# A gated linear recurrence feeding a two-layer perceptron: the first 512 steps as two units of 256

## The chip, the cores and the metric

The kernel runs on one core of one Trainium2 chip. The metric is the device time of one execution in microseconds (us). The engines are named as the profile names them: PE is TensorE (PEld its weight loads), DVE is VectorE, ACT is ScalarE, POOL is GpSimd, SP is SyncE; SP, ACT and POOL also issue DMAs. Each engine runs its own instructions strictly in order.

## The reference

For each of 4 sequences and 8 heads, a state of 48 x 48 complex numbers decays by a complex gate of at most 0.999 in magnitude and takes up k v^T; q reads the real part. The result, as 3072 rows of 384, goes through a perceptron with squared ReLU.

```python
mag = np.sqrt(a_re * a_re + a_im * a_im)
scale = np.minimum(mag, 0.999) / (mag + 1e-06)
a_re_n, a_im_n = (a_re * scale, a_im * scale)
for t in range(S):                      # S = 768
    new_re = ar * S_re - ai * S_im
    new_im = ar * S_im + ai * S_re
    S_re, S_im = (new_re + k v^T, new_im)
    y[t] = q[t] @ S_re
h = x @ w_in                            # x: (3072, 384), w_in: (384, 2048)
r = np.maximum(h, 0.0)
out = (r * r) @ w_out                   # w_out: (2048, 384)
```

The two weight matrices arrive as 64-bit floats and are converted on the chip.

## The kernel before

**Blocks.** The 3072 steps are six blocks of 512 (`L`). A block's gates a, and its q and k, lie in `aq[z]`, z being the half of the heads, with four consecutive steps in each of the 128 partitions. For each block the same stages follow.

1. *Chain* (`chain`). `roots` and `normalise` scale the gates (ACT: square, logarithm, exponential; DVE: the rest). `inner` multiplies up the gates of a partition's four steps, three rounds of products per half (L1006, L1014); the last product is `xn`. `totals` turns `xn` so that the partitions lie along the free dimension (PE, L1040), `scan` forms the running products over the 128 partitions (DVE, many small instructions, L1065 to L1175), and `back` turns the result back. `rest`/`apply` multiplies it into each step, takes the inverse by logarithm and exponential, and writes the scaled q and k (L1241 to L1306). In block 0 some sums of `apply` are made by PE in PSUM (`both`, table `HOMES`).
2. *Pairs* (`pairs`). For each of four pairs of heads: q and k are turned (PE transposes and ACT evictions in block 0 and for three pairs of block 1, otherwise DVE and DMA), `score` makes masked products of chunks of 128 steps (PE, DVE mask at L1443), `keep` carries the states (L1468, L1482), `mix` sums the output (L1499, L1503), which ACT and DMAs put into `xT`. `gather` brings the scaled k into chunk order by DMA (L1342).
3. *Dense* (`dense`), for two groups of 256 steps. First layer L1550 with `w1`, ReLU and square on ACT, second layer L1598 with `w2`; `(0,0)`, `(0,1)` and `(1,0)` in this plain form, later groups with seven products in place of eight (`seven`, L1660), and block 5 with a similar scheme in the first layer (`eleven`).

**Weights.** `piece`, `fetch` and `convert` bring eight raw pieces of w1 and eight of w2 (768 KB each) into whatever memory is still free (`raw1`, `raw2`), and ACT (L839, L844) and DVE (L846 to L853) convert them to 32 bits.

**Order of the work.** Every operation is a step with an engine, a duration that the program assumes, keys that it reads and writes, and a rank. `Plan` places the steps by a list schedule over all engines and emits each engine's instructions in that order; at run time each engine keeps its order and waits on semaphores. Ranks say who goes first among what is ready: chain of block n `(CHAIN, n)` = (2, n), its pairs (1, n), conversions (2, 0.3) and (2, 0.6), dense (3, n). From block 1 on the chain's and pairs' steps off DVE come ahead of everything.

The numbers that set up block 0 and the conversions:

```python
FINE = [(0, 0), (0, 1), (1, 0), (1, 1)]
BY_PE = [(0, i) for i in range(NP)] + [(1, i) for i in range(3)]
rank = (W2, 0.6) if i >= NPIECE else (W1, 0.3)
```

Of the kernel before, what the change touches and what calls it, by code (L numbers as in the profile page):

```python
# [603 lines left out]
def fast_path(ctx, tc, q, k, v, a_re, a_im, moe_w_in, moe_w_out, out, flag):  # L604
# [6 lines left out]
    C = 128  # L611
    W = 4
    L = W * C
    NU = B * S // L
# [16 lines left out]
    FINE = [(0, 0), (0, 1), (1, 0), (1, 1)]  # L631
# [6 lines left out]
    BY_PE = [(0, i) for i in range(NP)] + [(1, i) for i in range(3)]  # L638
# [55 lines left out]
    ok = sb("ok", NU * 4).rearrange("p (n j) -> p n j", n=NU)  # L694
# [37 lines left out]

    def vs(n):
        return n % 2 if n < ROOM else 0

# [29 lines left out]
    def fk(z, *qs, ps=(0, 1)):  # L765
        return [("f", z, q_, p) for q_ in qs for p in ps]
# [4 lines left out]

    CHAIN, PAIR, DENSE, CONV, LATE = 2, 1, 3, 3, 5
    W1, W2 = 2, 2

# [14 lines left out]
    def two(t):  # L789
# [9 lines left out]
    tkeys = [[("QT", 2, 0), ("QT", 2, 1)], [("QT", 2, 0), ("QT", 2, 1), ("A", 2)], [("v", 1)]]  # L799
# [3 lines left out]
    raw2 = [w2slot(3), q2, v1,  # L803
            (QT[0].bitcast(U32)[:, 0:2 * PW], [("QT", 0, 0), ("QT", 0, 1)]),
            (QT[1].bitcast(U32)[:, 0:2 * PW], [("QT", 1, 0), ("QT", 1, 1)]),
            w2slot(3), q2, v1]
# [20 lines left out]
    def convert(i):  # L827
        held = tuple(plan.wrote[("a", 1)][1]) if SOON <= i < NPIECE else ()
# [4 lines left out]
        rank = (W2, 0.6) if i >= NPIECE else (W1, 0.3)  # L833
# [22 lines left out]
    def inspect(i):  # L856
# [6 lines left out]
        if i == 0:  # L863
            step("POOL", 0.2, xk(NU - 1, range(NM)), [("gate", 1)],
                 lambda: pool.tensor_copy(out=gate[:, 0:NM],
                                          in_=xT[:, (NU - 1) % 2, :, L - 1]), rank)
# [13 lines left out]
    def parts(n):  # L880

        t, got = n * L, []
        while t < (n + 1) * L:
            b, s = divmod(t, S)
            m = min(S - s, (n + 1) * L - t)
            got.append(((t - n * L) // W, m // W, b, s))
            t += m
        return got

    def places(i):  # L890
        return [(CH, 0, CH), (0, CH, CH)] if i % 2 else [(0, 0, C)]

    def load(n):
        rank = (CHAIN, n)
        for half, name, pair in ((0, "a", (a_re, a_im)), (1, "qk", (q, k))):
            for z in range(2):
                t = aq[z][:, half * Z:(half + 1) * Z].rearrange(
                    "p (r h x) -> p r h x", r=2, h=HH)
                late = []
                if half and (n == 1 or n > 2):  # L900
                    late = xk(n - 1, [NM - 1])
                split = n == z == half == 0
                for x, j, ap in [(x, j, ap) for x in range(1 + split) for j, ap in enumerate(pair)]:
                    hs = slice(x * HH // 2, (x + 1) * HH // 2) if split else slice(0, HH)
                    for p0, m, b, s in parts(n):
                        src = ap[b, z * HH + hs.start:z * HH + hs.stop, s:s + m * W, :].rearrange(
                            "h (p c) d -> p h (c d)", c=W)
                        queue = sp if n else pool if half else (sp, act)[j]
                        dma(queue, late if n or not half else [("gate",)],
                            [(name, z)] + [(name, z, "r", j, y) for y in ([x] if split else [0, 1])  # L910
                                           if n == 0],
                            lambda t=t, p0=p0, m=m, j=j, src=src, queue=queue, hs=hs:
                            queue.dma_start(out=t[p0:p0 + m, j, hs], in_=src),
                            rank, *((m * 3072, 4.0) if n else (m * 2765 // (1 + split), 2.25)),
                            group=n)
            if n == 0 and half == 0:
                for z in range(2):
                    step("POOL", 0.2, [("a", z)], [("gate",)],
                         lambda z=z: pool.tensor_copy(out=gate[:, z:z + 1],
                                                      in_=aq[z][:, Z - 1:Z]), rank)  # L920
        t = vv[vs(n)].rearrange("p (i h d) -> p i h d", i=W, h=H)
        for i in range(W):
            b, s = divmod(n * L + i * C, S)
            src = v[b, :, s:s + C, :].rearrange("h t d -> t h d")
            vrank = (CHAIN, 1) if n == 1 else (DENSE, 20 + n if n else 6)
            for p0, t0, m in places(i):
                dma(pool, [("gate", 2)] if n == 2 else xk(n - (vs(n) == vs(n - 1)), [NM - 1])
                    if n else [("gate",)],
                    [("v", vs(n))], lambda i=i, p0=p0, t0=t0, m=m, src=src: pool.dma_start(
                        out=t[p0:p0 + m, i], in_=src[t0:t0 + m]), vrank,  # L930
                    m * 1536 * (1 if n else 1.9), 4.0 if n else 2.9, group=n)

    def chain(n):
# [89 lines left out]
        if n == 0:  # L1023
            fill(FILLS[0], ("a", 1))
# [934 lines left out]
```

## Time and profile before

| | |
|---|---|
| runs of the kernel | 668.84 and 669.37 us, median 669.11 |
| the profiled execution | 669.86 us; span 668.1 us from first to last instruction |
| granted TensorE clock, mean | 0.975 |
| busy: PE, DVE, ACT, POOL | 630.8, 574.1, 347.3, 116.8 us |
| PE waits in the first 44 us | 16.8, 9.1 and 2.8 us, each for DVE's `xn` |
| first dense matmuls of block 0, steady from | 84.7 us |
| first dense matmuls of block 1 | 192.1 us |
| DMA | 80.35 MB, 120 GB/s on average |

Busy times of engines overlap; an engine that is not the bottleneck may idle at no cost. PE's busy time includes short gaps between matmuls, since matmul ends are modelled, and each 32-bit matmul stands as two records (a transpose as one). In a row of the timeline stand the start, the busy time of the group, the engine, the line and operation, out<-in, the shapes and the count; in brackets the idle time ahead of it and what ended it.

### The profile page before, as it was taken

The page shows a single profiled execution, that of the slowest core. Times are in us where ns is not written, and L with a number is a line of the kernel's source. Part 1 is how long each engine was busy: PE and PEld are TensorE (multiplying, and loading weights), DVE is VectorE, ACT ScalarE, POOL GpSimd, SP SyncE. Part 2 cuts the span into 40 slices and gives each one's busy share as a digit, 9 for nine tenths or more (in the row PEclk, how much of TensorE's full clock was granted, in tenths as well). Part 3 has the DMA queues.
Part 4 walks back from the last instruction along what each step waited for, and adds up shares of the span by engine and source line. Part 5 has one row for each costly group of instructions (what it writes and reads, how often), then busy time and mean ns, then how long its engine had stood idle before and what let it go on. Part 6 is the DMA issues. An engine that isn't in the chain of part 4 may idle for free.

```text
span 668.1 us, 11941 instructions
## 1 busy us (share of the span) xinstructions
PE 630.8 (94%) x4414; PEld 551.9 (83%) x4414; DVE 574.1 (86%) x1147; ACT 347.3 (52%) x600; POOL 116.8 (17%) x192
## 2 busy tenths in 40 slices
PE   3259999999999999999999999999999999999996
PEld 3237886787778689999988999988999989988996
DVE  7999997898798898798989898989879989659971
ACT  7948979775656262448353358263367352045400
POOL 7401040402000021040021040111040111032200
PEclk8569999999999999999999999999999999999999
DMA  6963686305530037560057580056470053377720
GB/s 194 322 239 69 147 248 154 71 1 156 135 90 1 12 87 186 131 174 6 7 129 174 132 179 0 14 118 164 122 178 1 25 123 95 81 228 239 255 95 29
DMA packets 54340, 80.35 MB, mean 120 GB/s; under 512 B 11200, under 2 KB 36896, under 8 KB 54272
## 3 DMA queue, kind: packets, MB, share of 16 engines
q0 software_dynamic: 15360, 42.51, 22.7%
q1 hardware_dynamic: 34448, 31.64, 18.5%
q10 hardware_dynamic: 4464, 5.35, 3.2%
q8 instruction: 37, 0.61, 0.4%
q14 instruction: 31, 0.25, 0.1%
HBM read 48.76 MB, written 4.72 MB: 80 GB/s over the span
## 4 chain that ended last, share of the span: by engine, by line
PE 91%; DVE 5%; ACT 1%; DMA 1%; issue 0%; SPq 0%; DVEq 0%
PE d L1550 29%; PE d L1660 25%; PE d L1598 9%; PE sc L1440 5%; PE tr L1468 4%; PE yp L1499 4%; PE yp L1503 3%; PE d L1795 2%; PE tr L1795 2%; PE sc L1550 2%; PE sc L1795 1%; PE tr L1040 1%; DMA aq<-in_a_re_dram 1%; PE d L1419 1%; PE tr L1419 1%; PE yp L1795 1%
## 5 line engine op out<-in xcount | busy, mean ns | idle before, releaser
L1550 PE MATMUL d<-xT,w 128*128 128x256 f32 x888 | 198.7, 381 | 0.0
L1550 PEld LDWEIGHTS d<-xT,w 128*128 128x128 f32 x888 | 166.7, 190 | 23.3 <-issue 0.7
L1583 ACT ACTIVATE g<-d 128x512 f32<-128x512 f32 x74 | 44.2, 598 | 90.8 <-PE d L1550 84.8
L1660 PE MATMUL d<-T,g 128*128 128x192 f32 x512 | 88.7, 328 | 0.0
L1660 PEld LDWEIGHTS d<-T,g 128*128 128x128 f32 x512 | 83.2, 190 | 1.1 <-issue 0.7
L1615 POOL DMA_DIRECT2D out_dram<-ot x40 | 25.6, 643 | 259.5 <-DVE ot L1685 162.3
L1660 PE MATMUL d<-w,g 128*128 128x192 f32 x384 | 68.1, 329 | 0.0
L1598 PE MATMUL d<-w,g 128*128 128x384 f32 x192 | 64.9, 489 | 0.0
L1660 PEld LDWEIGHTS d<-w,g 128*128 128x128 f32 x384 | 62.3, 190 | 1.5 <-issue 0.9
L1342 POOL DMA_DIRECT2D KC<-f x52 | 28.1, 557 | 151.8 <-DVE f L1306 124.8
L1598 PEld LDWEIGHTS d<-w,g 128*128 128x128 f32 x192 | 35.6, 190 | 22.1 <-issue 0.2
L1584 ACT ACTIVATE g<-g 128x512 f32<-128x512 f32 x80 | 50.6, 633 | 2.6
L1676 DVE TENSOR_TENSOR g<-g 128x512 f32<-128x512 f32 x64 | 43.2, 685 | 7.0 <-PE d L1660 6.3
L1241 DVE TENSOR_TENSOR f<-aq,xn 128x384 f32<-128x384 f32 (+1 forms) x64 | 46.0, 752 | 1.8 <-ACT xn L1186 1.8
L1393 DVE STREAM_TRANSPOSE aq<-f 128x384 f32<-128x384 f32 (+1 forms) x51 | 42.7, 914 | 0.3
L1440 PEld LDWEIGHTS sc<-QT 96*64 96x64 f32 x736 | 33.3, 137 | 5.1 <-issue 3.2
L1006 DVE TENSOR_TENSOR f<-aq 128x384 f32<-128x384 f32 x72 | 37.0, 554 | 0.6
L1440 PE MATMUL sc<-QT 96*64 96x128 f32 (+1 forms) x736 | 36.7, 250 | 0.2 <-ACT QT L1423 0.2
L1443 DVE TENSOR_TENSOR A<-sc,mask 128x512 f32<-128x512 f32 x45 | 29.7, 683 | 7.4 <-PE sc L1440 7.2
L1685 DVE TENSOR_TENSOR ot<-ot,d 128x192 f32<-128x192 f32 x63 | 21.3, 350 | 14.5 <-PE d L1660 14.0
L1272 ACT ACTIVATE f<-aq 128x1536 f32<-128x1536 f32 (+1 forms) x14 | 16.9, 1208 | 24.5 <-DVE aq L1258 24.4
L1499 PE MATMUL yp<-A,v 128*48 128x128 f32 x312 | 29.6, 277 | 0.0
(274 smaller groups left out, 1107.9 us busy)
## 6 DMA issues: line engine op xcount, KB each, us to landing
QT<-aq SPq DMA_DIRECT2D x136, 64.0 KB, 2.0
f<-in_moe_w_in_dram POOLq DMA_DIRECT2D x8, 768.0 KB, 6.3
f<-in_moe_w_out_dram POOLq DMA_DIRECT2D x8, 768.0 KB, 6.7
QT<-aq ACTq DMA_DIRECT2D x68, 64.0 KB, 2.1
out_dram<-ot POOLq DMA_DIRECT2D x40, 96.0 KB, 3.6
KC<-f POOLq DMA_DIRECT2D x36, 96.0 KB, 3.5
xT<-yt SPq DMA_DIRECT2D x34, 96.0 KB, 2.8
T<-in_moe_w_out_dram POOLq DMA_DIRECT2D x4, 768.0 KB, 11.2
```

The lines of the kernel that those rows point to most:

```text
L1006: lambda c=c, j=j: dve.tensor_tensor(out=f[:, j], in0=a[:, :, :, c - 1], in1=a[:, j, :, c].unsqueeze(1).to_broadcast([C, 2, HH, D]), op=AL ...
L1241: lambda j=j, r=r: dve.tensor_tensor(out=f4[:, j, r], in0=a[:, r], in1=over(j), op=ALU.mult), rk)
L1393: lambda src=src, dst=dst: dve.transpose(out=dst, in_=src), rank)
L1440: pe.matmul(sa[p0:p0 + CH, j, t0:], lhsT=T[:, j, 1, h, t0:t0 + CH], rhs=T[:, j, 0, h, t0:], start=True, stop=True)
L1499: pe.matmul(ps[64 * h:64 * h + D, j - js[0]], lhsT=v5[:, j, 2 * i + h], rhs=aa[h][:, j], start=True, stop=at[j] is None)
L1550: pe.matmul(ps, lhsT=w1[:, f // FP, m, ts(f % FP, C)], rhs=xT[:, n % 2, m, ts(grp, G)], start=(m == 0), stop=(m == NM - 1))
L1583: act.activation(out=o, in_=ps, func=AF.Relu)
L1584: act.activation(out=o, in_=o, func=AF.Square)
L1598: pe.matmul(ps, lhsT=gt[:, f % 2, ts(i, C)], rhs=w2[:, f], start=(f == 0), stop=(f == NF - 1))
L1660: pe.matmul(bank[b][:, 0:DH], lhsT=gsets[x][h][:, j - HW * h, r], rhs=w(j), start=first and j == 0, stop=last and j == NT - 1)
L1676: lambda: dve.tensor_tensor(out=g[:, :, o], in0=g[:, :, x0], in1=g[:, :, x1], op=op),
L1795: pe.matmul(ps[:, jj], lhsT=u[:, ts(jj, C)], rhs=v_, start=i == 0, stop=i == len(terms) - 1)
```

## The change

Block 0 becomes two *units*, 0 and 1, of 256 steps; blocks 1 to 5 are units 2 to 6. `UNITS` holds each unit's first step and its steps per partition, 2 for the first two units and 4 for the others. Unit 0 and unit 1 each have their own loads, roots, products in the lanes (one round in place of three), totals, scan, turning back, apply, turns, scores and states, all of half width but for the totals, the scan and the turning back, whose tiles do not depend on the unit's length. Only unit 0 has PSUM homes. Loads of a, q and k read runs of two steps (384 bytes) in place of four (768). Dense group (0,0) follows unit 0's pairs, group (0,1) those of unit 1; the groups keep their 256 steps. Block 1's roots keep two of their columns in `TT`, so that they needn't wait for `ff`.

The raw w2 pieces 3 and 4 go to the second half of `xT` and the second third of `TT` in place of `QT[0]` and `QT[1]`, and w2's conversions get the rank (2, 0.12), that is ahead of unit 1's chain.

```diff
+    R1, R2 = 0.3, 0.12
+    UNITS = [(0, 2), (L // 2, 2)] + [(L * i, W) for i in range(1, NB)]
+    NU = len(UNITS)
+    FIRST_ = 2
-    FINE = [(0, 0), (0, 1), (1, 0), (1, 1)]
+    FINE = [(0, 0), (0, 1), (1, 0), (1, 1), (2, 0), (2, 1)]
-    BY_PE = [(0, i) for i in range(NP)] + [(1, i) for i in range(3)]
+    BY_PE = [(n, i) for n in range(FIRST_) for i in range(NP)] + [(2, i) for i in range(3)]
...
     raw2 = [w2slot(3), q2, v1,
-            (QT[0].bitcast(U32)[:, 0:2 * PW], [("QT", 0, 0), ("QT", 0, 1)]),
-            (QT[1].bitcast(U32)[:, 0:2 * PW], [("QT", 1, 0), ("QT", 1, 1)]),
-            w2slot(3), q2, v1]
+            (xT[:, 1].rearrange("p m t -> p (m t)").bitcast(U32), xk(1, range(NM))),
+            q3, w2slot(3), q2, v1]
...
-        rank = (W2, 0.6) if i >= NPIECE else (W1, 0.3)
+        rank = (W2, R2) if i >= NPIECE else (W1, R1)
...
+    def home_of(n):
+        w = UNITS[n][1]
+        z = 2 * HH * w * D
+        return w, z, z // 2, 2 * z * n if n < FIRST_ else 0
...
     def chain(n):
-        rank = (CHAIN, n)
-        A = [aq[z][:, 0:Z] for z in range(2)]
+        u = blk(n)
+        W, Z, Y, off = home_of(n)
+        rk0 = (0, 0.15)[n] if n < FIRST_ else u
+        rank = (CHAIN, rk0)
+        A = [aq[z][:, off:off + Z] for z in range(2)]
...
+        away = n == FIRST_
+        if away:
+            for z in range(2):
+                col[z][2:] = [TT[:, (2 * z + x) * Y:(2 * z + x + 1) * Y] for x in range(2)]
...
-        spare = ["sc0", "sc1", "tr0", "tr1"][:4 - 2 * n] if n < EARLY and grp == 0 else []
+        spare = ["sc0", "sc1"] if n < EARLY and grp == 0 else []
...
-        for grp in range(2):
-            (seven if n == NU - 1 else dense)(n, grp)
+        for grp in [n] if n < FIRST_ else range(2):
+            (seven if u == NB - 1 else dense)(u, grp)
```

How it moves instructions is shown at two places. The first is PE around the totals of block 1, the transposes of `xn` by `perm` (L1040 before, L1098 now; L1598 and L1684 are the second layer, L1550 and L1636 the first, L1588 and L1592 `mix`). Before:

```order
L1598 MATMUL d_113<-w_67,g 128x384 x2
L1598 MATMUL d_111<-w_67,g 128x384 x2
L1040 MATMUL tr_116<-perm,xn 128x16x8 x3
L1040 MATMUL tr_117<-perm,xn 128x16x8 x3
L1598 MATMUL d_111<-w_67,g 128x384 x2
L1550 MATMUL d_112<-xT,w_66 128x256 x3
```

Now:

```order
L1684 MATMUL d_112<-w_67,g 128x384 x2
L1588 MATMUL yp<-A_87,v_78 48x128
L1588 MATMUL yp<-A_88,v_78 48x128
L1592 MATMUL yp<-QT_75,S_86 48x128 x2
L1588 MATMUL yp<-A_87,v_78 48x128
L1588 MATMUL yp<-A_88,v_78 48x128
L1592 MATMUL yp<-QT_75,St_90 48x128 x2
L1636 MATMUL d_110<-xT,w_66 128x256 x6
L1636 MATMUL d_111<-xT,w_66 128x256 x3
L1098 MATMUL tr_115<-perm,xn 128x16x8 x3
L1098 MATMUL tr_116<-perm,xn 128x16x8 x3
```

Before, the totals stand inside the second layer of group (0,0), of which two matmuls are left. Now that layer stands between unit 1's pairs and is used up, then come unit 1's last `mix`, nine matmuls of group (0,1), and the totals.

The second place is DVE at the end of unit 1's scan (L1221, L1226), which didn't exist before (L866, L870 and L873 convert a raw piece, out<-raw; L1301 is the first row of unit 1's apply):

```order
L866 TENSOR_SCALAR w_66<-xT 128x768
L873 ISA w_66<-xT,w_66 128x1536
```

and ten rows on:

```order
L873 ISA w_66<-T,w_66 128x1536
L866 TENSOR_SCALAR w_67<-xT 128x768
L873 ISA w_67<-w_67 128x1536
L866 TENSOR_SCALAR w_67<-T 128x768
L870 SCALAR_TENSOR_TENSOR w_67<-T,w_67 128x768
L873 ISA w_67<-T,w_67 128x1536
L1301 TENSOR_TENSOR f_70<-aq_68,xn 128x192 x5
```

`w_66` is w1 and `w_67` w2. The raw piece of w1 in `xT` is converted inside the scan, and twelve rows later a raw piece of w2 is read from the same place; conversions of w2, which stood between block 1's roots before, stand ahead of unit 1's apply.

More of the change, by code (lines that the diff above doesn't have):

```diff
@@ L942, in chain @@
-        ahead = (CHAIN, n - 0.01)
-        late = [rank, (CHAIN, n + 0.1) if n == 0 else rank]
+        u = blk(n)
+        W, Z, Y, off = home_of(n)
+        rk0 = (0, 0.15)[n] if n < FIRST_ else u
+        early = n < FIRST_
+        rank = (CHAIN, rk0)
+        A = [aq[z][:, off:off + Z] for z in range(2)]
+        QK = [aq[z][:, off + Z:off + 2 * Z] for z in range(2)]
+        fu = [f[:, off:off + 2 * Z] for f in ff]
+        col = [[fu[z][:, s * Y:(s + 1) * Y] for s in range(4)] for z in range(2)]
@@ new lines, in chain @@
+        key = partial(fk, n=n)
+        away = n == FIRST_
+        if away:
+            for z in range(2):
+                col[z][2:] = [TT[:, (2 * z + x) * Y:(2 * z + x + 1) * Y] for x in range(2)]
+        room = [("QT", 2, h, x) for h in range(2) for x in range(2)] + [("A", 2, x) for x in range(2)]
+        room = room * away
+        first = (CHAIN, 0.25) if u == 1 else (CHAIN, rk0 - 0.02) if early else rank
+        ahead = (CHAIN, rk0 - 0.01)
+        late = [rank, (CHAIN, rk0 + 0.1) if early else rank]
@@ L1120, in side @@
         def side(n_, src, reads, dst, writes, after=()):
-            if n:
+            if not early:
                 step("DVE", tt(n_), reads, writes, lambda: dve.tensor_copy(out=dst, in_=src), ahead,
```

326 lines of the change are left out of this document (189 added, 137 removed).

## The prediction

> **What bounds the kernel now.** First the page: its second line of busy times and the slices, to see which engine is full and where it is not.
>
> ```profile
> PE 630.8 (94%) x4414; PEld 551.9 (83%) x4414; DVE 574.1 (86%) x1147; ACT 347.3 (52%) x600; POOL 116.8 (17%) x192
> PE   3259999999999999999999999999999999999996
> DVE  7999997898798898798989898989879989659971
> ```
>
> TensorE (PE) is full from the fourth slice on (16.7 us each), VectorE (DVE) from the first. So the span is a start in which DVE works and PE mostly waits, then about 600 us of PE. Next the waits of PE in the whole run, which say what the start consists of:
>
> ```profile
> PE tr L1040 <- DVE xn L1014: 19.6, 2, 16.8
> PE tr L1040 <- DVE xn L1168: 9.3, 2, 9.1
> ```
>
> Both are waits for DVE's first chain: roots and products of block 0 (L1014), then its scan (L1168). After them PE waits for nothing longer than 0.7 us before the kernel's last 30 us. Third, the busy times by stretches (PE, PEld, DVE, ACT, POOL; the second figure of each "busy (x)" is a count):
>
> ```profile
> 30.70:43.00 12.30, 3.23 (x21) 2.80 (x19) 11.32 (x42) 8.32 (x15) 2.93 (x4) 0.78 1.03 313
> 43.00:77.10 34.10, 32.89 (x320) 26.20 (x321) 33.47 (x78) 26.51 (x48) 4.35 (x8) 0.93 0.36 90
> 77.10:103.40 26.30, 26.30 (x191) 22.94 (x188) 25.82 (x43) 21.57 (x33) 9.22 (x12) 1.00 0.85 221
> 103.40:125.60 22.20, 22.20 (x76) 13.78 (x75) 17.93 (x27) 19.26 (x29) 2.99 (x4) 1.00 0.39 103
> 125.60:160.00 34.40, 34.40 (x176) 27.30 (x175) 32.19 (x94) 22.85 (x46) 6.31 (x11) 1.00 0.21 46
> ```
>
> DVE is full up to 103 us and nearly so to 160, while PE is full too from 43 on. The two meet at four places, read in the timeline:
>
> ```profile
> 84.71 1.99 PE L1550 MATMUL d<-xT,w 128*128 128x256 f32 x8
> 125.01 0.63 DVE L1014 TENSOR_TENSOR xn<-f 128x192 f32<-128x192 f32 x2
> 125.31 0.88 PE L1040 MATMUL tr<-perm,xn 128*128 128x128 f32 x6
> 192.13 2.86 PE L1550 MATMUL d<-xT,w 128*128 128x256 f32 x12
> ```
>
> Dense work runs steadily from 84.71. DVE ends block 1's products xn at 125.6, and PE turns them at 125.31, half of them before the other half is written: DVE arrives just in time. From there PE is busy without a gap to 192.13, where block 1's own dense layer begins. So up to 125.3 the start has two bounds of the same height, and DVE has this slack in it:
>
> ```profile
> 106.99 0.96 DVE L973 SCALAR_TENSOR_TENSOR f<-f 128x768 f32<-128x768 f32 x1 [3.56 <-ACT f L968]
> ```
>
> **The change, part by part.** It halves the latency to the first dense matmul and adds DVE work ahead of block 1's xn. Both are worked out.
>
> *What comes earlier.* Block 0's xn needs, with half the steps, the same instructions at half the width. One of 384 elements starts 0.47 us after the last, one of 192 0.27 us (the fence below); the first chain ends at 28.1 now. By the new order the DVE rows to unit 0's xn sum to 12.6 us against 23.2 at the same place now, that is 17.5 us with the same 4.9 us of landings and waits around them. Its scan then ends at about 36 instead of 42.98 (unit 1's roots stand between its rows), and its apply, at half width, at about 57 instead of 77.1. First dense matmuls come near 60, steady ones near 64: 20 us earlier than 84.7.
>
> *What is added on DVE.* The rows that carry it:
>
> ```profile
> 27.53 0.63 DVE L1014 TENSOR_TENSOR xn<-f 128x192 f32<-128x192 f32 x2
> 76.62 0.55 DVE L1306 TENSOR_TENSOR f<-aq 128x384 f32<-128x384 f32 x1
> 20.32 1.96 DVE L1006 TENSOR_TENSOR f<-aq 128x384 f32<-128x384 f32 x4
> 22.20 0.90 DVE L1014 TENSOR_TENSOR aq<-f 128x192 f32<-128x192 f32 x3
> 30.68 0.13 DVE L1065 MEMSET e<- 128x3 f32 x2
> 38.83 0.55 DVE L846 TENSOR_SCALAR w<-g 128x768 uint32<-128x768 uint32 x1
> 42.98 0.54 DVE L1241 TENSOR_TENSOR f<-aq,xn 128x384 f32<-128x384 f32 x1
> 45.94 1.49 DVE L1241 TENSOR_TENSOR f<-aq,xn 128x384 f32<-128x384 f32 x3
> 66.92 0.68 DVE L1443 TENSOR_TENSOR A<-sc,mask 128x512 f32<-128x512 f32 x1
> 67.52 0.95 DVE L853 CUSTOM_DVE_ANT_0 w<-g,w 128x1536 uint16<-128x1536 uint16 x1
> ```
>
> - A second scan. Its tiles have 128 partial products whatever the unit's length, so nothing in it is halved: 42.98 - 30.68, less 0.5 for the conversion at 38.83, is 11.8 us. Lower bound: its rows at 0.07 us + 1 us per 960 elements (what 0.47 and 0.27 give) are 9.2 us; the rest is drain between dependent rows, into which the new order puts conversions. I take **10.5**.
> - Products inside the lanes (L1006, L1014): three rounds become one in each of two units, 12 of 0.47 and 12 of 0.27 now, 8 and 8 then: **-3.0**.
> - Apply (L1241 to L1306): 51 instructions at 0.47 become 107 at 0.27, five of them new because unit 1 has no PSUM homes: 24.0 to 28.9, **+4.9**.
> - Masks (L1443): 8 of 0.60 become 16 of 0.33 by the same slope, **+0.5**; small rows (few, ce, lv) **+0.3**. Roots and normalise come out even: unit 1 squares on ACT.
>
> Sum 13.2 us. The 3.6 us wait at 103.4 should go, since block 1's roots now start from squares that ACT has long made: -3.6. Net **+9.6 us**, so block 1's xn at 135.2. Between bounds: 9.2 for the scan gives +8.3; 11.8 and a wait that only moves gives +14.5.
>
> *Does PE have to wait for it?* The new order (shown with the change) says so. All of group 0's second layer is used up between unit 1's pairs, and only nine matmuls stand between the last pair and block 1's totals (L1098).
>
> PE is in order: behind those nine it stands until DVE has written xn. Its own work up to there is 41.6 us of dense (48 matmuls at 0.43, 32 at 0.65, rows below), 3 of turns, and half of block 0's four pairs, which now last from 55.29 to 84.71, so 14.7 at most:
>
> ```profile
> 55.29 2.13 PE L1419 MATMUL d<-ident,f 128*96 128x128 f32 x16
> ```
>
> From 62 on that is 121 with no wait, well under 135. So DVE sets the place, and the 20 us are lost again.
>
> *What PE makes up.* Before the totals it has done nine matmuls of group 1 and all of the second layer, against three and 30 of 32 now. One costs 0.43 us (two records of 0.216, the row at 127.32) or 0.65:
>
> ```profile
> 127.32 10.52 PE L1550 MATMUL d<-xT,w 128*128 128x256 f32 x48
> 187.68 2.85 PE L1598 MATMUL d<-w,g 128*128 128x384 f32 x8
> 191.81 0.39 PE L1503 MATMUL yp<-QT,St 96*48 96x128 f32 x4
> ```
>
> That is 6 x 0.43 + 2 x 0.65 = 3.9 us less to do afterwards, if block 1's pairs come no slower than now. But now they need the whole 66.8 us from 125.3 to 192.13, with second-layer matmuls put in while a pair is not ready, up to 187.68; the last mix ends 0.1 us before block 1's dense. With less filler PE waits for pairs. Between 0 and 3.9 I take **-1.5**. After 192 PE is full whatever happened before, so a delay there stays.
>
> *The raw weights' new homes.* The last w2 pieces now use w2's own fourth slot, xT's second half and T, each free only after the piece in it is converted. DVE is in order, and these conversions (L866 to L873) stand ahead of unit 1's apply. Between freeing and the row that reads the next piece lie 5.4 us of DVE rows for w2's slot and for xT, and 7.1 for the last one in T. A fetch lands this much after its issue, on quiet queues late in the kernel and on busy ones at 88 us:
>
> ```profile
> f<-in_moe_w_out_dram POOLq DMA_DIRECT2D x8, 768.0 KB, 6.7
> QT<-in_moe_w_out_dram POOLq DMA_DIRECT2D x2, 768.0 KB, 9.0
> ```
>
> With about 1 us for the issue, quiet landings leave DVE waiting 2.3, 0 and 0.6 us (a wait at the first covers the second), busy ones 4.6, 0 and 2.9. From 0 (rows with drains last longer than their sum) to 7.5 I take **+2.0**.
>
> *Other parts.* Twice as many evictions of turned q and k on ACT cost some 2 us of ACT, which has 7.6 us free in 43 to 77: nothing, and 2 us if ACT leads. The dense groups stay as they are.
>
> Loads of a, q and k of units 0 and 1 read runs of 384 bytes instead of 768. Now the early ones take this long:
>
> ```profile
> aq<-in_a_im_dram ACTq DMA_DIRECT2D x1, 384.0 KB, 6.9
> 8.43 0.84 ACT L954 ACTIVATE f<-aq 128x768 f32<-128x768 f32 x1 [0.35 <-DMA aq<-in_a_re_dram]
> ```
>
> With half the bytes I expect the third square (L954 at 8.43) near 6.5; at worst, at half the rate, it stays at 8.4 and the first chain ends 2 us later. [...] No row here shows runs of 384 B apart.
>
> **Sum.** 669.86 us (the profiled execution, span 668.1) + 9.6 - 1.5 + 2.0 = 680.0; the median of the runs shown is 0.75 below the profiled one, so **679.2 us** is the forecast, 1.5% slower. Bounds of this case: 669.1 + 8.3 - 3.9 = 673.5 and 669.1 + 14.5 + 7.5 = 691.
>
> **The rivals.** *The start shrinks (not slower).* If DVE's extra rows fill drains and waits so that xn comes at 126 or earlier, PE's own path decides: its real work starts 7 us earlier (36 for 43), with 1.5 us of added turns and 3.3 us in which group 1 waits for the last pair's xT. 669.1 - 7 + 1.5 + 3.3 = **667**. For it: PE's 29 us of waits at the start. Against: DVE's 33.5 busy of 34.1 us from 43 to 77. Chance 0.20.
>
> *Late fetches (slower by over 2%).* If the three fetches land as on busy queues, DVE stands 7.5 us instead of 2.0 ahead of unit 1's apply, and xn, totals and all of PE behind them move with it: **685**; it decides from 682.5 on, that is from 5.3 us of such waits, seen as DVE waiting for a DMA at L866. For it: block 1's a, q and k are loaded in the same 20 us. Against: five of the eight w2 pieces are clear of it. Chance 0.27.
>
> *It doesn't do what it says*, that is, dense still starts near 84: the order excludes it, since half-width rows stand ahead of it on DVE.
>
> **How the numbers follow.** Forecast 0.53, start shrinks 0.20, late fetches 0.27. Range 665 to 690: it leaves out the lower part of the first rival and the far end of the other. Within 2% (655.7 to 682.5, about what a measurement tells from no change) lie nine tenths of the forecast and of the first rival, and a seventh of the second: same 0.69, slower 0.27, faster 0.04.
>
> **What would show it.** Right: steady L1636 near 64 us; two scans on DVE of some 12 to 18 us each; PE waiting for xn (L1098 <- DVE xn) near 130; totals of block 1 near 137, and block 1's first dense near 202. Wrong: totals before 128 (DVE did not bind), or a first dense matmul after 70. The fetches are told by L866's waits: over 5 us is the second rival, none takes 2 us off.

## The result and the profile after

The change makes the kernel slower: 693.25 us (median of 691.61 and 694.90) against 669.11, a ratio of 1.036 (95% interval 1.025 to 1.047). Run again beside the experiments it took 688.89 us, a ratio of 1.030 (1.028 to 1.031). The forecast was 679.2, with 665 to 690 as its range: the direction held, the size did not, and block 1's totals, forecast near 137 us, came at 145.5. The second median lies just inside the range, but no step of the sum comes out better by it: xn and the totals were no earlier in its trace (143.3 and 146.2).

The page of the profiled execution (691.61 us) first, its busy times and slices, 17.2 us each:

```profile
span 689.9 us, 12197 instructions
PE 641.1 (93%) x4426; PEld 558.5 (81%) x4426; DVE 587.6 (85%) x1258; ACT 357.5 (52%) x671; POOL 118.3 (17%) x196
PE   1588889799998999999999999999999999999995
DVE  7999899969969789888999788998898989649971
```

TensorE (PE) is busy earlier than before, as intended, but its slices three to six are 8s, the eighth a 7 and the thirteenth an 8: there are holes where the kernel before, from its fourth slice on, had none. Of the 21.8 us of span, 10.3 are more busy time of PE (630.8 to 641.1) and 11.5 are more idle time. Four of PE's waits name the holes (engine, line, what for: total us, times, longest; one more of 2.1 us, for a mask at L1528, comes up in the last section):

```profile
PE tr L1098 <- DVE xn L1072: 12.4, 2, 10.2
PE d L1636 <- DMA xT<-yt: 10.5, 2, 5.3
PE tr L1098 <- ACT junk L1268: 8.4, 1, 8.4
PE tr L1497 <- DVE f L1367: 2.0, 1, 2.0
```

The first and third are the old waits of the start, shorter than before (20.8 us for 28.9). The second is new. It stands twice, once at the end of each unit; the timeline shows where (start, us, instruction, and in brackets the idle time ahead of it):

```profile
65.36 1.46 PE L1636 MATMUL sc<-xT,w 128*128 128x256 f32 x6
72.01 8.00 PE L1636 MATMUL d<-xT,w 128*128 128x256 f32 x24 [5.20 <-DMA xT<-yt]
133.00 1.13 PE L1636 MATMUL d<-xT,w 128*128 128x256 f32 x4
139.42 6.27 PE L1636 MATMUL d<-xT,w 128*128 128x256 f32 x14 [5.28 <-DMA xT<-yt]
145.52 0.82 PE L1098 MATMUL tr<-perm,xn 128*128 128x128 f32 x6
212.57 0.80 PE L1636 MATMUL d<-xT,w 128*128 128x256 f32 x1
```

After a unit's last pair PE has some dense matmuls left that need the first two row tiles of xT, and then stands until the last mix is evicted, sent and landed. The 14 records behind the second wait take 0.45 us each instead of 0.22. The windows say why; the column behind POOL's is PE's granted clock:

```profile
66.80:72.00 5.20, 0.01 (x1) 0.02 (x1) 4.92 (x13) 3.31 (x9) 0.00 (x0) 0.85 1.01 278
72.00:74.00 2.00, 1.99 (x5) 1.64 (x6) 1.72 (x12) 2.00 (x6) 0.91 (x2) 0.50 1.12 235
139.40:141.40 2.00, 1.98 (x5) 1.64 (x6) 1.45 (x4) 0.00 (x0) 0.00 (x0) 0.50 1.11 171
143.40:145.50 2.10, 2.10 (x6) 1.56 (x5) 0.00 (x0) 1.03 (x2) 0.00 (x0) 0.50 1.06 153
145.50:150.00 4.50, 4.50 (x25) 4.05 (x24) 2.96 (x12) 3.29 (x9) 0.00 (x0) 1.00 0.88 166
```

Behind the two waits PE's granted clock was 0.50, for 5.2 and 6.1 us. From the totals on (145.52) to block 1's own dense layer (212.57) go 67.05 us; before it was 66.8. So what the change costs is decided before 145.5.

VectorE (DVE) ends block 1's xn a little earlier than that:

```profile
140.25 0.63 DVE L1072 TENSOR_TENSOR xn<-f 128x192 f32<-128x192 f32 x2
```

It is 15.2 us later than before (125.6), where +9.6 were forecast. Here is VectorE's work up to that point, in groups of its lines. Each row of its timeline is counted from its start to the next one's start, without the waits, so drains are in it (in the scan of the kernel before, 0.59 us from a row of 384 elements to the one that reads its result, at 31.26, for 0.47 us to one that doesn't, at 30.79):

```
us up to block 1's xn      before       after     difference  forecast
scan                       12.1 (x43)   23.8 (x86)   +11.7     +10.5
apply                      25.3 (x51)   31.8 (x107)   +6.5      +4.9
inside the lanes           19.5 (x48)   14.9 (x40)    -4.6      -3.0
masks                       4.8          6.0          +1.2      +0.5
roots and normalise        24.3         25.0          +0.7       0
conversions                26.1         25.3          -0.8       0
small rows, states, rest    6.0          5.8          -0.2      +0.3
waits (with 1.0 to begin)   7.7          8.3          +0.6      -3.6
```

The rows that carry it, from the groups by line (busy us, mean ns, then idle time ahead and its releaser), first of before, up to 125.6 us:

```profile
L1241 DVE TENSOR_TENSOR f<-aq,xn 128x384 f32<-128x384 f32 x16 | 8.2, 550 | 0.2 <-ACT xn L1186 0.2
L1443 DVE TENSOR_TENSOR A<-sc,mask 128x512 f32<-128x512 f32 x8 | 5.3, 684 | 0.0
L973 DVE SCALAR_TENSOR_TENSOR f<-f 128x768 f32<-128x768 f32 (+1 forms) x5 | 4.0, 797 | 4.3 <-ACT f L968 4.3
```

and of the changed kernel, up to 140.9:

```profile
L1301 DVE TENSOR_TENSOR f<-aq,xn 128x192 f32<-128x192 f32 x32 | 9.6, 352 | 0.2 <-ACT xn L1244 0.2
L1528 DVE TENSOR_TENSOR A<-sc,mask 128x256 f32<-128x256 f32 x16 | 6.4, 418 | 2.0 <-PE sc L1524 2.0
L1221 DVE TENSOR_TENSOR KC<-e,yt 128x768 f32<-128x768 f32 x4 | 3.8, 954 | 1.2 <-ACT yt L1183 1.1
```

The wait for ScalarE (ACT) at the roots (4.3 us) did go. But 2.0 us of waits for PE's scores and 2.2 for ScalarE's small copies in unit 1's scan took its place, so the waits as a whole did not shrink. The copies were late because of PE: in ScalarE's order they stand behind rows that wait for the first dense matmuls of group (0,0), which PE began late, at half clock (0.50 from 72 to 77 us), after its first wait for xT. One of the two cases:

```profile
75.80 0.60 ACT L1669 ACTIVATE g<-d 128x512 f32<-128x512 f32 x1 [1.80 <-PE d L1636]
76.97 0.20 ACT L1183 COPY tx<-yt 128x24 f32<-128x24 f32 x1
77.20 0.53 DVE L1153 TENSOR_TENSOR KC<-yt,tx 128x144 f32<-128x144 f32 x2 [1.07 <-ACT tx L1183]
```

So a wait of PE also reaches VectorE's rows ahead of block 1's xn.

### The profile page after: what moved, and what is told of

Same layout as the page of the kernel before. It is cut to its first block, busy times and chain, and to the rows that moved or that the text cites. A ratio compares the mean times of both kernels' runs of the same rounds, so it can differ in the third digit from the quotient of the medians.

```text
span 689.9 us, 12197 instructions
## 1 busy us (share of the span) xinstructions
PE 641.1 (93%) x4426; PEld 558.5 (81%) x4426; DVE 587.6 (85%) x1258; ACT 357.5 (52%) x671; POOL 118.3 (17%) x196
## 3 DMA queue, kind: packets, MB, share of 16 engines
q10 hardware_dynamic: 4464, 4.95, 3.0%
## 4 chain that ended last, share of the span: by engine, by line
PE 84%; DVE 9%; DMA 4%; issue 1%; ACT 1%; SPq 0%; ACTq 0%; DVEq 0%
PE d L1636 28%; PE d L1746 24%; PE d L1684 8%; PE sc L1524 5%; PE tr L1556 4%; PE yp L1588 3%; PE yp L1592 2%; PE d L1877 2%; DMA xT<-yt 2%; DMA aq<-in_a_im_dram 2%; PE tr L1877 2%; PE sc L1877 1%; PE tr L1497 1%; PE tr L1098 1%; PE sc L1636 1%
## 5 line engine op out<-in xcount | busy, mean ns | idle before, releaser
L1636 PE MATMUL d<-xT,w 128*128 128x256 f32 x912 | 209.6, 389 | 10.5 <-DMA xT<-yt 10.5
L1636 PEld LDWEIGHTS d<-xT,w 128*128 128x128 f32 x912 | 175.7, 195 | 35.7 <-issue 11.9
L1684 PE MATMUL d<-w,g 128*128 128x384 f32 x192 | 68.7, 500 | 0.4 <-DVE w L873 0.4
L1684 PEld LDWEIGHTS d<-w,g 128*128 128x128 f32 x192 | 35.2, 194 | 19.8 <-DVE w L873 0.7
L1301 DVE TENSOR_TENSOR f<-aq,xn 128x192 f32<-128x192 f32 (+2 forms) x80 | 47.3, 632 | 3.3 <-ACT xn L1244 3.3
L1524 PE MATMUL sc<-QT 96*64 96x128 f32 (+1 forms) x736 | 38.1, 251 | 0.4 <-ACT QT L1501 0.3
L1528 DVE TENSOR_TENSOR A<-sc,mask 128x512 f32<-128x512 f32 (+1 forms) x54 | 31.7, 609 | 7.5 <-PE sc L1524 7.2
L1064 DVE TENSOR_TENSOR f<-aq 128x384 f32<-128x384 f32 x68 | 35.0, 554 | 0.6
L1333 ACT ACTIVATE f<-aq 128x1536 f32<-128x1536 f32 (+2 forms) x18 | 18.3, 1014 | 28.5 <-DVE aq L1319 28.5
L1601 ACT COPY yt<-yp 112x512 f32<-112x512 f32 (+1 forms) x24 | 12.5, 520 | 35.8 <-PE yp L1592 35.7
```

The costliest lines, as they stand in the source:

```text
L1064: lambda c=c, j=j: dve.tensor_tensor(out=f[:, j], in0=a[:, :, :, c - 1], in1=a[:, j, :, c].unsqueeze(1).to_broadcast([C, 2, HH, D]), op=AL ...
L1301: lambda j=j, r=r: dve.tensor_tensor(out=f4[:, j, r], in0=a[:, r], in1=over(j), op=ALU.mult), rk,
L1524: pe.matmul(sa[p0:p0 + CH, j, t0:], lhsT=T[:, j, 1, h, t0:t0 + CH], rhs=T[:, j, 0, h, t0:], start=True, stop=True)
L1528: step("DVE", tt(n_), [(b,)], ak_(a, x), lambda: dve.tensor_tensor(out=A0[:, 0:n_].rearrange("p (j o t) -> p j o t", o=2, t=C), in0=bank[b ...
L1636: pe.matmul(ps, lhsT=w1[:, f // FP, m, ts(f % FP, C)], rhs=xT[:, n % 2, m, ts(grp, G)], start=(m == 0), stop=(m == NM - 1))
L1684: pe.matmul(ps, lhsT=gt[:, f % 2, ts(i, C)], rhs=w2[:, f], start=(f == 0), stop=(f == NF - 1))
```

## The experiments

Four theories were set against each other. **A**: two chains of nearly the same height lie ahead of block 1's totals, VectorE's rows up to xn and PE's wait for xT with the half clock behind it. **B**: the second scan is the cost and PE only follows VectorE. **C**: the two waits for xT with their half clock are the cost. **D**, added after the first four kernels below: a raw piece of w2 that lands late holds ScalarE, which converts it in order, and so unit 1's scan, which waits for copies behind it. Unless said otherwise, a kernel has the same instructions in the same order as the changed one. All were timed beside the kernel before (668.9 to 669.1 each time). "Less" and "more" are against the changed kernel's 688.89 us.

### The changed kernel again

> The changed kernel again, as the yardstick for the runs beside it. All theories: 690 to 695 us, two waits of TensorE for the transfer into xT of about 5 us each (the first dense layer, L1636), granted clock 0.5 for some 5 us behind each, block 1's totals near 145.5 us and its xn on VectorE near 141 us.

688.89 us, a little under the 690 to 695 expected. The waits for xT were 6.2 and 5.1 us, xn ended at 143.3, totals began at 146.2. The profiled execution (691.69 us) is 2.8 us longer than the median, and the six executions of this kernel lie between 688.35 and 694.90 us. From one to the next the start moves: by the count above VectorE's rows up to xn are the same in this trace (132.8 us, for 132.6), but its waits are 10.5 us in place of 8.3. Differences below 2 us between single traces are therefore not read, a trace is set against a trace and not against a median, and medians that differ from 688.89 by 1 to 2 us are not clear of this spread, since that median is of four executions, taken beside the first three edited kernels alone.

### Unit 1's scan cut

```
- both products over all columns, xb.to_broadcast([C, 2, 4, 96]), own[0], own[1]
+ the same, [..., 0:1] in unit 1's scan (L1153, L1157, L1221, L1226)
```

> Left out: unit 1's second scan is computed for one column only (its output is not the reference's). All instructions stay, in the same order, but those 36 rows on VectorE shrink from 11.7 us to about 3.5. Theory A (two chains of nearly the same height: VectorE's rows up to block 1's xn, at 140.9, and TensorE's wait for xT with the half clock behind it, up to 145.5): TensorE's waits at 92 to 98 us (2.4) and the slow matmuls behind them (1.1) go, the rest of TensorE's work up to the wait for xT stays, so totals near 142 and the time 3 to 5 us less, about 689. Theory B (the second scan on VectorE is the cost and TensorE only follows): 8 us less, about 685. Theory C (only the two waits for xT with their half clock cost): no change beyond 1 us, 692.

Without these products the kernel's own test at the end sends it through its second, general path, so its total (2307 us) says nothing; the rows up to that test do. The test's result on VectorE, of the changed kernel and of this one:

```profile
666.76 0.14 DVE L1943 TENSOR_SCALAR flag<-tr 1x1 int32<-1x1 f32 x1
...
663.23 0.14 DVE L1964 TENSOR_SCALAR flag<-tr 1x1 int32<-1x1 f32 x1
```

3.5 us less, within A's 3 to 5, and not B's 8. But not for A's reason: xn also came only 3.4 us earlier (139.9 for 143.3), though the scan rows shrank by 7.1 us, from 23.8 to 16.7 for both units. VectorE's own waits took the other half:

```profile
DVE KC L1173 <- ACT yt L1203: 5.0, 2, 4.3
DVE w L866 <- DMA xT<-in_moe_w_out_dram: 1.9, 1, 1.9
```

The second is the wait that the prediction's second rival named. In the changed kernel it was hidden under the scan. The first is the same thing by another way: here ScalarE stood 3.5 us at L859 for a raw piece, and the copy that VectorE waited 4.3 us for is behind it in its order. In the changed kernel ScalarE stands at the same place:

```profile
71.63 0.91 ACT L859 ACTIVATE T<-T 128x768 uint32<-128x768 uint32 x1 [1.83 <-DMA T<-in_moe_w_out_dram]
```

That gave theory D. In the changed kernel itself the piece costs the scan less: nothing in the trace above, whose two waits for copies are PE's doing, and 1.2 us in the second trace, where ScalarE stood 2.8 us.

### No wait for xT in group 1

```
- rhs=xT[:, n % 2, m, ts(grp, G)]
+ rhs=xT[:, n % 2, min(m, 1) if n == 0 and grp == 1 else m, ts(grp, G)]
```

> Left out: group 1 of block 0 reads row tile 1 of xT where it should read tile 2 (its output is not the reference's), so it need not wait for the last transfer into xT; same instructions in the same order. Theory A: the wait of 5.3 us at 134 and some 3 us of half clock go from TensorE's chain, but VectorE's xn at 140.9 is next, with a new wait there: 2 to 5 us less, about 689, totals near 141. Theory B: the same, at most 4.6 less. Theory C: 8.5 us less, about 684, totals near 137.

687.39 us, 1.5 less: under A's 2 to 5 us, and far from C's 8.5. The intervals of the two ratios overlap (1.026 to 1.029 and 1.028 to 1.031), so the medians alone don't show a gain; between the traces the end of the totals moves up by 2.4 us (147.0 to 144.5) and the execution is 1.9 us shorter (689.80 for 691.69). PE no longer waits for xT and at once meets the other chain:

```profile
136.10 4.15 PE L1636 MATMUL d<-xT,w 128*128 128x256 f32 x18
140.44 0.33 PE L1098 MATMUL tr<-perm,xn 128*128 128x128 f32 x1 [0.19 <-DVE xn L1072]
143.76 0.76 PE L1098 MATMUL tr<-perm,xn 128*128 128x128 f32 x5 [3.00 <-DVE xn L1072]
```

The 18 records take 4.15 us with the granted clock at 1.00. Then PE waits 3.0 us for the second half of xn, and the clock falls behind that wait too: 0.74 from 143.7 to 145.7 us, 0.50 from there to 147.7.

### Both

> Left out: both of the above, and group 0 also reads tile 1 for tile 2. Same instructions in the same order. Theory A: both chains shrink, so more than the sum of the two alone: 11 to 15 us less, 678 to 682, totals near 132, set by VectorE's xn. Theory B: 8 us less as with the cut scan alone, 685. Theory C: 16 us less, the two waits with their half clocks, 677, and as much with the scan left whole.

Again only the rows up to the kernel's test are comparable: the flag stands at 661.44 for 666.76, 5.3 us less. A had said 11 to 15, B 8, C 16; all missed. xn ended at 139.9, exactly as with the cut scan alone, and totals waited for it. What held xn was D's: VectorE waited 4.6 us for ScalarE's copies and 2.2 for the raw piece in xT.

### The wait filled

```
+ if n == 0 and grp == 1, once: 40 (then 20) x pe.matmul(bank["sc0"][:, 0:C], lhsT=ident, rhs=ident)
  ahead of the first matmul that needs row tile 2 of xT
```

> The changed kernel with 40 matmuls of ident by ident put ahead of the first dense matmul that waits for xT of unit 1 (134 us), into a free bank; nothing left out. They fill the wait of 5 us and keep the granted clock at 1.0, so the 14 matmul records behind it take 3.0 us, not 4.7 to 6.3. Theory C (the waits for xT with their half clock are the cost): 2 to 3 us less than the changed kernel's 688.9, so 686. Theory A (VectorE's xn of block 1 lies right below): block 1's totals move up only to xn's end, 0.5 to 3 us less than 145.5 to 146, and the time goes down by as much, 686.5 to 688.5. Theory B: no change.

691.41 us, 2.5 more. The 40 matmuls took 9.2 us, 4 longer than the wait, and the totals came at 147.2. So the size was wrong, and the run was made again with half:

> As e4_fill, with 20 matmuls instead of 40 (4.6 us at the 0.115 us of a record measured there, two records each), so that they end before the transfer lands. The records behind the wait take 0.22 us each instead of 0.33 to 0.45, 2 to 3 us less in all. Theory A: totals move up until xn's end (141 to 143) stops them: 1 to 3 us under 688.9. Theory C: 2 to 3 us less. If the half clock is worth nothing: 688.9.

688.70 us, no change. By the medians none of the theories came. In the traces the clock stayed up (1.00 in four windows between 136 and 146 us) and the totals moved from 146.2 to 143.7, with xn's end at 142.4:

```profile
134.50 4.73 PE L1640 MATMUL sc<-ident 128*128 128x128 f32 x40
140.60 3.26 PE L1643 MATMUL d<-xT,w 128*128 128x256 f32 x14 [0.51 <-DMA xT<-yt]
```

The 14 records take 3.26 us here, against 6.27 and 4.67 in the two traces without the fill. So the half clock costs 1.4 to 3.0 us at this place. The traced execution is 3.4 us shorter than the changed kernel's (688.33 for 691.69), the medians are the same; whether the fill gains anything is open.

### The transfer into xT with less beside it

```
- queue.dma_start(out=t[p0:p0 + m, j, hs], in_=src)
+ None if n == 2 and half else queue.dma_start(...)      (q and k of block 1)
```

> Left out: block 1's q and k are not loaded (1.5 MB, issued at 134 us, as the last piece of unit 1 is on its way into xT), what lies there is used; the kernel's own test is told that all is well. If the transfer into xT is slow because it shares the DMA engines with these loads, it takes 2.5 to 3.5 us instead of 5.8, TensorE's wait falls from 5.1 to 2 or 3 us, the granted clock stays near 1, TensorE reaches the totals near 140 and waits for xn (141 to 143): 2 to 4 us under 688.9. If the transfer is slow by itself (evict, issue and landing in a row): no change in it, 688 to 690.

689.39 us, no change. The last piece took 4.6 us from issue to landing instead of 5.6, where 2.5 to 3.5 were expected:

```profile
xT<-yt ACTq DMA_DIRECT2D x1, 48.0 KB, 5.6
...
xT<-yt ACTq DMA_DIRECT2D x1, 48.0 KB, 4.6
```

PE's wait fell from 5.1 to 4.1 us and the 14 records behind it still took 4.95 us, for the 3.26 with the wait filled by 20; the totals came at 146.1. So q and k are at most a small part of the transfer's time: the difference of 1 us, between one trace each, is within the spread. v was still loaded beside it, so how quick it would be alone was not tried.

### No late fetches

```
- lambda: pool.dma_start(out=t, in_=src)
+ lambda: None if i >= NPIECE + 3 else pool.dma_start(out=t, in_=src)
```

> Left out: the last five raw pieces of w2 are not fetched, what lies in their homes is converted instead, and the kernel's own test of its sums at the end is told that all is well (its output is not the reference's). Same instructions and order otherwise. Theory D (a third chain of the same height: a raw piece lands late, ScalarE's conversion of it waits, unit 1's scan waits for ScalarE's copies behind it): VectorE's 3.4 us of waits in that scan go, apply of unit 1 starts 2 to 3 us sooner, transfers into xT are shorter by 1 to 2 us: 3 to 6 us less than 688.9. Theories A to C alone: 0 to 2 us less.

687.72 us, 1.2 less, under the 3 to 6 of theory D and within the spread. In the trace VectorE's waits in unit 1's scan are gone, its apply starts at 87.2 instead of 91.3 and xn ends at 138.8 instead of 143.3. That is not D alone, since PE's first wait for xT, which had held ScalarE's copies, fell as well, from 6.2 to 2.1 us. And PE still waits 4.9 us for xT in group 1, and the 14 records behind it take 0.43 us each:

```profile
136.91 6.07 PE L1636 MATMUL d<-xT,w 128*128 128x256 f32 x14 [4.87 <-DMA xT<-yt]
142.82 0.82 PE L1098 MATMUL tr<-perm,xn 128*128 128x128 f32 x6
```

So the totals come 4.0 us behind xn, 3.3 earlier than in the changed kernel's trace for the 4.5 that VectorE gains, and this execution is 3.3 us shorter than that one (688.41 for 691.69). That the medians are only 1.2 apart is the spread between executions.

### No late fetches, scan cut

> Left out: the last five raw pieces of w2 are not fetched, unit 1's second scan is computed for one column only, and the kernel's own test of its sums is told that all is well. Same instructions (but the five transfers) and order. Theory A with D (three things of nearly the same height ahead of block 1's totals: VectorE's rows, the raw pieces that hold unit 1's scan by way of ScalarE, and TensorE's wait for xT with its half clock): VectorE's xn falls to about 131, apply of unit 1 starts 6 to 8 us sooner than without the cut, but TensorE's two waits for xT stay, so totals near 138 to 139 and the time 4 to 6 us under 688.9, 683 to 685. Theory B (the scan is the cost, TensorE follows VectorE): xn's whole 12 us, 677. Theory C (only the waits for xT): 688.

683.68 us, 5.2 less, within A and D's 683 to 685. The places were missed: xn, expected at about 131, ended at 138.1, and the totals, expected at 138 to 139, began at 142.5, behind a wait for xT of again 5.1 us. The profiled execution was 3.9 us longer than the median (687.62).

### All three taken away

> Left out: what the last kernel leaves out, and block 0's dense layer reads tile 1 of xT for tile 2 in both groups, so that TensorE waits for no last transfer. Theory A with D: now totals follow xn, 130 to 132, and the time is 13 to 16 us under 688.9, 673 to 676; what is left over the kernel before (669.1) is the apply in halves and the masks, some 5 us. Theory C: 16 us less than 688.9, 673, but then nearly all of it also without the cut scan, against e2_no_xt_wait_1 (1.5 us). Theory B: as e9.

681.49 us, 7.4 less, more than any one of them (1.2, 1.5, and 3.5 for the scan by its trace), but not the 13 to 16 expected. The totals follow xn, at last at the same point:

```profile
132.87 0.62 DVE L1072 TENSOR_TENSOR xn<-f 128x192 f32<-128x192 f32 x2
136.18 0.63 DVE L1072 TENSOR_TENSOR xn<-f 128x192 f32<-128x192 f32 x2
136.59 0.77 PE L1098 MATMUL tr<-perm,xn 128*128 128x128 f32 x5 [2.99 <-DVE xn L1072]
```

xn is still 11.2 us later than in the kernel before. By the same count as above: what is left of the second scan 4.6, apply 7.1, masks 1.2, roots 0.6, waits 3.1, less 4.6 inside the lanes and 0.9 of conversions. What the edits take away lies ahead of unit 1's apply. From the first row of that apply to the end of block 1's xn VectorE needs 52 us in each kernel:

```
                     apply starts   xn ends   between
changed kernel           88.8        140.9      52
the same again           91.3        143.3      52
scan cut                 87.9        139.9      52
no late fetches          87.2        138.8      52
those two                85.8        138.1      52
all three                84.5        136.8      52
```

This kernel also shows theory D by itself: it differs from the one with both edits (above) in the fetches, and in what the kernel's test is told. xn ends 3.1 us earlier (136.8 for 139.9).

### The w2 conversions later

```
- R1, R2 = 0.3, 0.12
+ R1, R2 = 0.3, 0.6
```

> The changed kernel with the rank of the w2 conversions set back from 0.12 to 0.6, which puts most of them behind unit 1's scan and apply but still ahead of block 1's xn, and leaves 8 second-layer and dense matmuls for TensorE behind unit 1's last pair. Nothing left out. Theory A (VectorE's sum of rows up to xn binds as well): xn stays within 2 us of 141 to 143, the wait for xT is filled, totals come with xn: 2 to 4 us less than 688.9. Theory C (the wait for xT): 6 to 8 us less, 682. Theory D (the raw pieces of w2 hold the scan of unit 1): xn earlier by 3 us or more, 4 to 7 us less.

695.80 us, 6.9 more: none of the theories. (Here the order does change.) Unit 1's apply began at 79.3, 12 us earlier, and PE had 36 dense matmuls for the place of the wait, which was gone. But the conversions now lie between apply and xn, which ended at 145.6, later than ever. PE's waits moved to the end of block 1's pairs, where the filler then lacked:

```profile
205.50 2.90 PE L1636 MATMUL d<-xT,w 128*128 128x256 f32 x6 [5.55 <-DMA xT<-yt]
217.71 4.68 PE L1636 MATMUL d<-xT,w 128*128 128x256 f32 x13 [2.73 <-DMA xT<-yt]
```

### A delay of xn alone, in the kernel before

```
- lambda c=c, j=j: dve.tensor_tensor(...)
+ lambda c=c, j=j: [dve.tensor_tensor(...) for _ in range(3 if n == 1 else 1)]
```

> The kernel before, with each of the 12 first products inside the lanes of block 1 (L1006) written three times instead of once: 24 more rows of 0.47 us on VectorE, 11.3 us, straight ahead of block 1's xn; same result, same order. It prices a delay of xn alone. The prediction's claim (VectorE sets block 1's totals, and what is late there stays): 669.1 + 11.3 = 680.4, and with the half clock behind a long wait of TensorE, about 3 us more, 683. Rival (TensorE has enough other work to take it in): below 675.

681.67 us, a ratio of 1.019 (1.017 to 1.020), between the 680.4 and 683 worked out from the profile of before. xn ended 10.2 us later, and the time rose by 12.6:

```profile
135.19 0.63 DVE L1014 TENSOR_TENSOR xn<-f 128x192 f32<-128x192 f32 x2
135.60 1.33 PE L1040 MATMUL tr<-perm,xn 128*128 128x128 f32 x5 [4.80 <-DVE xn L1014]
136.72 2.77 PE L1598 MATMUL d<-w,g 128*128 128x384 f32 x4
```

The 4 records behind the wait take 0.69 us each instead of 0.36 in the kernel before, and the granted clock averages 0.72 from 130 to 140 us: that adds to the delay itself. With xn 11.2 us late, the kernel with all three taken away also lost 12.6 us against before. That the two agree to a tenth is chance, since its clock did not fall behind the totals' wait (1.00 from 133.6 to 146 us); that a late xn costs about its own length holds in both.

Set side by side, the traces with a comparable end show where the time is decided (us; the last column is the time of the profiled execution less the end of block 1's totals):

```
                     xn ends   totals end    time    difference
before                125.6      126.2      669.9      543.7
xn delayed            135.8      136.9      682.8      545.8
all three             136.8      137.4      680.7      543.3
no late fetches,
  scan cut            138.1      143.3      687.6      544.3
no late fetches       138.8      143.6      688.4      544.8
no wait for xT        144.0      144.5      689.8      545.3
filled, 20            142.4      144.5      688.3      543.8
changed kernel        140.9      146.3      691.6      545.3
later w2              145.6      146.7      694.7      548.0
no q and k            143.9      146.9      690.6      543.7
changed, again        143.3      147.0      691.7      544.7
filled, 40            142.1      148.0      691.7      543.8
```

From the end of block 1's totals to its own end every kernel but one needs 543 to 546 us; the exception, with w2's conversions later, waits for xT twice more behind that point. So the loss is the lateness of the totals. They end 0.5 to 1.1 us behind xn where PE waits for xn (or just meets it), and 2.1 to 5.9 us behind it where PE's wait for xT, or what fills it, ends last.

## Why the prediction was wrong, point by point

**That VectorE bounds the start, and that a late xn stays to the end: right of the kernel before, half right of the changed one.** The delay of xn alone showed it, in the kernel before, with no part of the change. In the changed kernel xn is late too, but it no longer ends last: PE's wait for xT does.

**That dense work comes some 20 us earlier and that this is lost again: right, but for the steady part.** The first dense matmul stood at 58.96 us, for 78.81 before; "steady near 64" was 72.0, 12.7 us earlier than before and not 20, since the wait for the first unit's xT came between.

**The term of VectorE's added rows: too small.** 13.2 us forecast, 14.6 measured. Second scan 11.7 (10.5 taken, 11.8 the bound), apply 6.5 (4.9 taken: rows that read a scalar, L1350 and L1354, go at 0.33 and 0.39 us and not 0.27), masks 1.2, roots 0.7; the rows inside the lanes gave back 4.6 instead of 3.0.

**The wait of 3.6 us subtracted: the step that failed on VectorE.** The wait itself went, as said. It was wrong to take all of VectorE's waits to shrink by that. New ones took its place, 2.0 us for PE's scores and 2.2 for ScalarE's copies, which were themselves held by PE's first wait for xT. 4.2 us of the forecast's 5.6 us of error in xn (+9.6, measured +15.2) is this term. The upper bound worked out for it, "a wait that only moves", with 14.5 us, was the case that came, and fell short by 0.7.

**What PE makes up, -1.5: the step that failed on PE.** It was read off the order that only nine matmuls stand between the last pair and the totals, and they were taken as work done in time. They are also the only cover of the last transfer into xT, which took 5.8 us from issue to landing (48 KB, first trace). With nine too few, PE stood 5.28 us and went on at a granted clock of 0.50, and the totals came 4.6 us behind xn instead of with it. The prediction had this wait, with 3.3 us, in its first rival, and left it out of its sum. Taking it away gave 1.5 us in the medians and 2.4 us of the totals in the traces, since xn is next.

**The raw weights' homes, +2.0: not far off in size, wrong in place.** VectorE never waits at L866 in the changed kernel. ScalarE waits for a piece, at L859, 1.83 us in the first trace and 2.8 in the second, and only in the second does the scan wait behind it, 1.2 us. Without the five fetches the median fell by 1.2 us, and with the scan cut and no wait for xT xn came 3.1 us earlier. The second rival (late fetches, 685) thus named a wait that was there, but not its place, and it carries little of the loss; the first (the start shrinks) fell with xn 15.2 us later.

**The loads in runs of 384 B** did not set the start. Half the bytes in runs of 384 B landed in 4.4 us, against 6.9 for the whole, and the third square began at 6.10, earlier than the 6.5 assumed:

```profile
aq<-in_a_im_dram ACTq DMA_DIRECT2D x2, 192.0 KB, 3.6
...
aq<-in_a_im_dram ACTq DMA_DIRECT2D x1, 192.0 KB, 4.4
...
6.10 0.52 ACT L1011 ACTIVATE f<-aq 128x384 f32<-128x384 f32 x1 [1.49 <-DMA aq<-in_a_re_dram]
```

Per byte that is a quarter to a third slower. A fixed part of 1.9 us in each of the two, an estimate from 6.9 and 4.4, would give the same figures at one rate, but 192 KB in runs of 768 B, the first row, from the kernel before, took 3.6 us, so at equal size the short runs took 0.8 us more, at another place in the queue. The prediction's worst case, half the rate, would by these figures have been 6.9 us, as long as for the whole. Why the short runs took longer no run shows.

**The sum** in the forecast's own terms, up to block 1's dense layer: xn +15.2 for +9.6, PE +5.2 for -1.5 (the totals began 0.3 us ahead of xn's end before and 4.6 behind it now, and from them to the dense layer it is 0.3 longer), the fetches, inside the first, for +2.0: 20.4 us for 10.1. The rest of the span, 1.4 us, was not traced to one place.

Still open: how the 7.4 us of all three divide. Each alone gave 1.2 to 3.5, and the changed kernel's executions differ by several us. Also open is whether the apply in halves alone costs what the count says; it was not run at full width.

## What to carry to other kernels

Splitting a unit to start sooner halves the work of each piece only where the rows scale with length; a scan over a fixed number of partial sums is simply done twice (23.8 us of rows for 12.1), and every wide row becomes two with a fixed part each (0.27 us from start to start at 192 elements, 0.47 at 384). When a planner has balanced a start, removing one wait shows the next within a few microseconds: list all chains that end at the same instruction, with their heights, before taking credit for a wait that goes. And matmuls that stand behind the last transfer of a unit are its cover: count them against that transfer's time from issue to landing (5.8 us here), not only as work done. Set the places in a trace against the time of that same execution, not against a median: executions of this kernel (688.35 to 694.90 us) differ by more than most of the edits were worth.

## What the runs showed of the hardware

The granted clock fell after some short waits too. Behind the waits of 5.2 and 5.3 us in the changed kernel it was 0.50 until about 77.2 (the window from 76 to 78 us averages 0.69) and 145.5, that is for 5.2 and 6.1 us after PE had begun again. A wait of 2.6 us (67.4 to 70.0 in the kernel without late fetches and with the scan cut) led to 0.50 as well, and so did one of 2.1 us before 209.4 in the changed kernel, some 1 us after PE had begun again:

```profile
207.30:209.40 2.10, 0.04 (x1) 0.07 (x2) 2.10 (x4) 2.04 (x5) 0.00 (x0) 1.00 0.95 253
209.40:211.00 1.60, 1.49 (x18) 1.23 (x20) 1.60 (x3) 0.50 (x1) 0.00 (x0) 0.80 0.80 244
211.00:212.60 1.60, 1.60 (x15) 1.24 (x11) 1.60 (x3) 0.00 (x0) 0.00 (x0) 0.50 0.38 122
```

A wait of 3.0 us in the kernel with all three taken away (133.6 to 136.6) did not lower it at all: it was 1.00 in every window up to 146 us. One of the same length in the kernel with no wait for xT in group 1 (140.8 to 143.7) led to 0.50. So the length of a wait alone doesn't say whether the clock falls; what else decides it no run shows.
